# Decode attention with a gated MLP on one core: wq's first load in eight interleaved transfers, K's first head in two halves, slots at multiples of 4096 bytes

## The chip, the cores and the metric

The kernel runs on 1 core of one Trainium2 chip. The metric is the device time of one execution in microseconds (us). Before the change it is 1366.23 us, the median of 3 runs (1365.65 to 1366.27).

## The reference, cut to what matters

One token (x, 576 wide) is normalized. From the result come two sums that are added to x: attention of 32 heads over a cache of 16384 keys and values of 128 floats each, and a gated MLP (4608 wide).

```python
def _A_ref(x, k_cache, v_cache, wq, wo):          # 32 heads, Sk = 16384, Dh = 128
    q = (x @ wq).reshape(B, Sq, H, Dh).transpose(0, 2, 1, 3)
    scores = jnp.einsum("bhqd,bhkd->bhqk", q, k_cache) * (Dh ** -0.5)
    p = _softmax(scores, axis=-1)
    o = jnp.einsum("bhqk,bhkd->bhqd", p, v_cache)
    return o.transpose(0, 2, 1, 3).reshape(B, Sq, H * Dh) @ wo

def _B_ref(x, w_gate, w_up, w_down):              # 576 -> 4608 -> 576
    h = _gelu(x @ w_gate) * (x @ w_up)
    return h @ w_down

xn = _layernorm(x)
return x + _A_ref(xn, k_cache, v_cache, wq, wo) + _B_ref(xn, w_gate, w_up, w_down)
```

All is float32. K and V are 8.39 MB per head each, 537 MB together; the weights are another 51 MB. Each byte is used once.

## The kernel before, in words

Three buffers of 64 KB per partition, `slot_a`, `slot_b` and `slot_v` (called `sa`, `sb`, `sv`), lie one behind the other in SBUF from byte 27904 (`SLOT_AT`) of each partition. Everything large passes through them. All large loads are issued on SP's queue, in the order of the program text; a load waits at SP until the buffer that it overwrites has been read.

Start. The very first instruction of SP loads rows 0 to 511 of wq into `slot_a` (L127): partition p receives rows 4p to 4p+3, which are 64 KB that lie together. It stands ahead of the rest of the program and raises the semaphore `ends` by 64; PE's first instruction waits for that (L222). Behind it SP issues the last 64 rows of wq (into `slot_b`, behind the place of w_gate's main part), the small pieces of w_gate and w_up (into `slot_v`), and w_gate's main part (into `slot_b`). ACT's queue loads x. DVE normalizes x; PE turns it into a column with five small products (into `pc`), and DVE spreads that column (`z`). `project` then multiplies x by wq: one step with the last rows, four steps with those in `slot_a`. ACT takes the first head's part of q (`qcur`), PE spreads it over all partitions, ACT copies it to `qs`. When PE has read `slot_a`, w_up's main part is loaded there. `ffn(0)` and `ffn(1)` do w_gate and w_up in the same way.

Heads. K of head 0 goes to `slot_b` as soon as w_gate has been used, K of head 1 to `slot_a` behind w_up, V of head 0 to `slot_v`. Then a loop on SP (L354 to L359) issues, for each head in turn, K two heads ahead (when DVE has signalled `s_kf`, that is, read a K) and V one head ahead (when PE has signalled `s_vf`). Each of these loads is 128 partitions of 64 KB.

Each engine has its own loop over the heads, coupled by semaphores. DVE, for each head (L376 to L389): wait for K (`s_k`) and for `qs` (`s_qd`), multiply K by `qs` in place (L382), tell ACT that `qs` may be overwritten (`s_qf`), sum over the 128 floats of each key (L384), tell SP that K is free (`s_kf`), and find the maximum with PE's help (L387, L389). ACT forms the exponentials; PE multiplies them with V in 32 groups (L361 on, recorded at L329), and signals `s_vf`. The heads alternate between `slot_b` (even) and `slot_a` (odd).

End. When K of head 30 has been used, 28 rows per partition of w_down go to `slot_b`; V of head 31, the rest of w_down and wo follow in pieces. DVE sums the first part of w_down, PE the rest and wo; the last small pieces of wo end the kernel.

The class `Order` keeps the books outside the loops: each instruction and each load is noted with the partitions and elements that it touches (`box`), and `needs` works out which semaphores a later one must wait for. `load` (L217; its transfers stand at L107 in the profile, other operations at L207, L210 and L215) makes a new semaphore for each load.

Of the kernel before, what the change touches and what calls it, by code (L numbers as in the profile page):

```python
# [10 lines left out]
ALU = mybir.AluOpType  # L11
AX = mybir.AxisListType

P = 128
H, SK, DH = 32, 16384, 128
D, DF = 576, 4608
R = SK // P
SUB = 64
DJ = 4
DM = P * DJ  # L20
# [12 lines left out]
WO_A = 20  # L33
WO_Q = 8
QUART = D // 4
SLOT_AT = 27904
SLOT_B = R * DH * 4


class Order:  # L40
# [15 lines left out]
        lo = ap.offset % row  # L56
        return ap.tensor.name, ap.offset // row, ap.offset // row + parts * max(1, pstep // row), lo, lo + sum(s * (n - 1) for s, n in free) + 1

    def needs(self, eng, reads, writes):
        need = {}  # L60
        for aps, is_write in ((reads, False), (writes, True)):
            for ap in aps:
                name, p0, p1, lo, hi = self.box(ap)
                for q0, q1, l, h, wrote, who, sem, value in self.log.get(name, ()):
                    if (wrote or is_write) and q0 < p1 and p0 < q1 and l < hi and lo < h:
                        if who == eng == "tensor":
                            continue
                        if self.seen[eng].get(sem, 0) < value and need.get(sem, 0) < value:
                            need[sem] = value
        self.seen[eng].update(need)  # L70
        return list(need.items())
# [29 lines left out]
        self.note(eng, self.sem[eng], value, reads, writes)  # L101

    def dma(self, dst, src, sem, value=16, eng="sync", out=False):
        need = self.needs(eng, [src] if out else [], [] if out else [dst])
        for s, v in need[:-1]:
            getattr(self.nc, eng).wait_ge(s, v)
        i = getattr(self.nc, eng).dma_start(dst, src)  # L107
        if need:
            i._wait_ge(*need[-1])
        i.then_inc(sem, 16)  # L110
        if value and not out:
            self.note("dma", sem, value, [], [dst])
# [5 lines left out]
@with_exitstack  # L118
def kernel(ctx: ExitStack, tc: tile.TileContext, x, k_cache, v_cache, wq, wo, wg, wu, wd, out):
    nc = tc.nc  # L120
    ends = tc.alloc_semaphore("ends")
    slots = []
    for i, name in enumerate(("slot_a", "slot_b", "slot_v")):
        t = nc.alloc_sbuf_tensor_at(name, [P, R * DH], F32, offset=SLOT_AT + i * SLOT_B)
        SIZES[t.name] = R * DH
        slots.append(t.ap())
    i = nc.sync.dma_start(slots[0], wq[:DM].rearrange("(p j) f -> p (j f)", j=DJ)).then_inc(ends, 64)  # L127
    tc.no_tile_sem_insts.add(i.ins.name)
    tc.add_to_no_dep_group("first", i.ins)
    tc.declare_fence(nc.sync.nop().ins, group="first")  # L130
    with tc.tile_critical(sync_engine=mybir.EngineType.SP):
        decode(tc, x, k_cache, v_cache, wq, wo, wg, wu, wd, out, slots, ends)
    tc.no_sync_barrier()
    nc.sync.wait_ge(ends, 64)
# [19 lines left out]
def decode(tc, x, k_cache, v_cache, wq, wo, wg, wu, wd, out, slots, s_ends):  # L154
    nc = tc.nc
    o = Order(tc)
# [3 lines left out]
    def sem():  # L160
        return tc.alloc_semaphore(f"d{next(names)}")

    def sbuf(name, *shape):
        n = 1
        for s in shape[1:]:
            n *= s
        t = nc.alloc_sbuf_tensor(name, [P, n], F32)
        SIZES[t.name] = n
        return t.ap()[: shape[0]]

    def psum(name, banks):
        t = nc.alloc_psum_tensor(name, [P, 512 * banks], F32)
        SIZES[t.name] = 512 * banks
        return t.ap()

    kv, vv = (c.rearrange("b h (p n) d -> p (b h) (n d)", p=P) for c in (k_cache, v_cache))
    xf = x.rearrange("b s d -> (b s) d")
    of = out.rearrange("b s d -> (b s) d")
    wmain = {n: w[:DM].rearrange("(p j) f -> p (j f)", j=DJ) for n, w in (("q", wq), ("g", wg), ("u", wu))}
# [4 lines left out]
    sa, sb, sv = slots  # L184
# [5 lines left out]
    qcur, qs = sbuf("qcur", 1, DH), sbuf("qs", P, DH)  # L190
    S = sbuf("scores", P, 2 * R)
# [3 lines left out]
    pm, nm, nb = sbuf("pm", P, 1), sbuf("nm", P, 1), sbuf("nb", P, 1)  # L195
    small = sbuf("small", P, 32)
    oT = sbuf("oT", P, WO_T)
    assert nc.sbuf_base <= SLOT_AT, nc.sbuf_base

# [3 lines left out]
    pt, pb, pc = pg[:, 512:1024], pg[:, 1024:], psum("pc", 1)  # L203
# [5 lines left out]
    def dve(name, out, *ins, **kw):  # L209
        o.op("vector", lambda e: getattr(e, name)(out, *ins, **kw), out, *[a for a in ins if isinstance(a, bass.AP)],  # L210
             *[a for a in kw.values() if isinstance(a, bass.AP)])
# [5 lines left out]
    def load(dst, src, **kw):  # L217
        o.dma(dst, src, sem(), **kw)
        return dst

    ROW3 = 3 * DF
    nc.tensor.wait_ge(s_ends, 64).then_inc(s_ends, -64)  # L222
    qt = load(sb[:, ROW3 : ROW3 + QS], wtail["q"])
    row3, tails, at = {}, {}, 0
    for n in "gu":
# [7 lines left out]
    for i in range(2):  # L233
# [6 lines left out]
    s_q, s_m, s_n, s_o, s_e, s_v, s_po, s_pq, s_pt, s_pb, s_pc, s_vf, s_kf, s_qf, s_qd, s_d, s_a = (  # L240
        tc.alloc_semaphore(f"h{n}") for n in range(17))
    s_k = [tc.alloc_semaphore(f"k{n}") for n in range(2)]
# [45 lines left out]
    def q_part(h):  # L288
        r, lo = 32 * (h // (H // 4)), h % (H // 4) * DH
        return qb[r : r + 1, lo : lo + DH]  # L290
# [41 lines left out]
    def take(e, s, n=1):  # L332
        e.wait_ge(s, n).then_inc(s, -n)  # L333

    def head(h):
        return bass.ds(h, 1)
# [6 lines left out]
    def load_k(h, dst, s):  # L343
        nc.sync.dma_start(dst, kv[:, head(h), :].rearrange("p h f -> p (h f)")).then_inc(s_k[s], 16)
# [1 line left out]
    def load_v(h):  # L346
        nc.sync.dma_start(sv, vv[:, head(h), :].rearrange("p h f -> p (h f)")).then_inc(s_v, 16)

    for h, dst in ((0, sb), (1, sa)):
        o.wait("sync", [], [dst])  # L350
        load_k(h, dst, h)
    o.wait("sync", [], [sv])
    load_v(0)
    with nc.sync.Fori(0, (H - 2) // 2) as i:  # L354
# [18 lines left out]
               for k in range(32)], s_po)  # L373
        nc.tensor.drain().then_inc(s_vf, 1)

    with nc.vector.Fori(0, H // 2):  # L376
        for s, kt in ((0, sb), (1, sa)):
            blk = kt.rearrange("p (n d) -> p n d", d=DH)
            sc = S[:, s * R : s * R + R]
            take(nc.vector, s_k[s], 16)  # L380
            take(nc.vector, s_qd)
            nc.vector.tensor_mul(blk, blk, qs.unsqueeze(1).to_broadcast([P, R, DH])).then_inc(s_d, 1)  # L382
            nc.vector.wait_ge(s_d, 1).then_inc(s_qf, 1)
            nc.vector.tensor_reduce(sc, blk, axis=AX.X, op=ALU.add).then_inc(s_d, 1)  # L384
            nc.vector.wait_ge(s_d, 2).then_inc(s_kf, 1)
            take(nc.vector, s_d, 2)
            nc.vector.reduce_max(pm, sc, axis=AX.X).then_inc(s_m, 1)  # L387
            take(nc.vector, s_pt)
            nc.vector.tensor_reduce(nm[:1], pt[:1, :P], axis=AX.X, op=ALU.max, negate=True).then_inc(s_n, 1)  # L389

    for h0, n in ((0, 6), (6, 8), (14, 8), (22, 8), (30, 2)):
        row, lo = divmod(min(h0 + 2, H - 1), H // 4)
        with nc.scalar.Fori(0, n) as i:
# [11 lines left out]
            src = q_part(min(h0 + 2, H - 1)) if n == 2 else qb[32 * row : 32 * row + 1, bass.ds(i * DH + lo * DH, DH)]  # L405
# [102 lines left out]
```

## Time and profile before

| | |
|---|---|
| median of 3 runs | 1366.23 us |
| the profiled execution | 1364.84 us |
| its span, first to last instruction | 1363.0 us |
| DVE busy | 1158.4 us (85%) |
| PE busy | 446.3 us (33%) |
| ACT busy | 67.8 us (5%) |
| read from HBM | 587.60 MB, mean 431 GB/s |
| K load, issue to landing (median) | 42.1 us |
| V load, issue to landing (median) | 29.1 us |

How to read it: the span is what the trace covers; the time is measured around it. A row of the timeline gives start, duration, engine, line and operation, output and inputs, and in brackets how long the engine was idle before and what ended that. A `q` behind an engine's name is its instruction queue: there an SP row is the issue of a transfer, not the transfer. In the view of stretches, each row has the stretch, its length, the busy time and number of instructions of PE, PE's weight loads, DVE, ACT and POOL, then the granted clock of TensorE, the DMA share and the rate.

### The profile page before, as it was taken

The page shows a single profiled execution, that of the slowest core. Times are in us where ns is not written, and L with a number is a line of the kernel's source. Part 1 is how long each engine was busy: PE and PEld are TensorE (multiplying, and loading weights), DVE is VectorE, ACT ScalarE, POOL GpSimd, SP SyncE. Part 2 cuts the span into 40 slices and gives each one's busy share as a digit, 9 for nine tenths or more (in the row PEclk, how much of TensorE's full clock was granted, in tenths as well). Part 3 has the DMA queues.
Part 4 walks back from the last instruction along what each step waited for, and adds up shares of the span by engine and source line. Part 5 has one row for each costly group of instructions (what it writes and reads, how often), then busy time and mean ns, then how long its engine had stood idle before and what let it go on. Part 6 is the DMA issues. An engine that isn't in the chain of part 4 may idle for free. (4 is left out here: it accounts for less than half of the span.)

```text
span 1363.0 us, 7778 instructions
## 1 busy us (share of the span) xinstructions
PE 446.3 (33%) x3012; PEld 161.7 (12%) x3012; DVE 1158.4 (85%) x193; ACT 67.8 (5%) x234; POOL 1.0 (0%) x7
## 2 busy tenths in 40 slices
PE   2431233333322333323222333333223333232236
PEld 1110101111111111101111111011011111011112
DVE  1049999999998888898888888998888888988882
ACT  0000000000000000000000000000000000000000
POOL 0000000000000000000000000000000000000000
PEclk9675666666556666665566666665566666655568
DMA  9999999999999999999999999999999999999998
GB/s 401 446 424 431 431 440 437 431 435 431 435 437 431 433 431 431 446 435 431 431 439 433 433 431 431 446 435 431 431 435 437 433 431 431 444 437 431 430 437 349
DMA packets 11683, 587.69 MB, mean 431 GB/s; under 512 B 1303, under 2 KB 1309, under 8 KB 1694
## 3 DMA queue, kind: packets, MB, share of 16 engines
q1 hardware_dynamic: 11668, 587.60, 99.7%
q8 instruction: 5, 0.08, 0.0%
q10 hardware_dynamic: 10, 0.01, 0.0%
HBM read 587.60 MB, written 0.00 MB: 431 GB/s over the span
## 5 line engine op out<-in xcount | busy, mean ns | idle before, releaser
L329 PE MATMUL po<-slot_v,pe 128*4 128x512 f32 x2048 | 291.7, 733 | 532.6 <-PEq L333 532.6
L382 DVE TENSOR_TENSOR slot_b<-slot_b,qs 128x16384 f32<-128x16384 f32 x16 | 275.6, 17226 | 38.0 <-DVEq L333 38.0
L382 DVE TENSOR_TENSOR slot_a<-slot_a,qs 128x16384 f32<-128x16384 f32 x16 | 275.6, 17226 | 30.6 <-DVEq L333 30.6
L384 DVE TENSOR_REDUCE scores<-slot_a 128x128 f32<-128x16384 f32 x16 | 275.5, 17220 | 2.3
L384 DVE TENSOR_REDUCE scores<-slot_b 128x128 f32<-128x16384 f32 x16 | 275.5, 17220 | 2.3
L329 PEld LDWEIGHTS po<-slot_v,pe 128*4 128x4 f32 x2048 | 56.2, 98 | 740.9 <-issue 740.9
L365 PE MATMUL pg<-ident,pm 128*1 128x128 f32 x32 | 11.9, 371 | 287.3 <-PEq L333 287.3
L329 PE MATMUL pc<-same,z 128*128 128x1 f32 x256 | 59.8, 355 | 0.0
L395 ACT ACTIVATE z<-po 128x512 f32<-128x512 f32 x32 | 19.1, 597 | 783.1 <-ACTq L333 783.1
L329 PEld LDWEIGHTS pc<-same,z 128*128 128x128 f32 x256 | 57.1, 328 | 0.5
L210 DVE TENSOR_TENSOR slot_v<-pg,same 128x396 f32<-128x396 f32 (+1 forms) x6 | 3.3, 558 | 51.9 <-PE pg L207 51.7
L365 PEld LDWEIGHTS pg<-ident,pm 128*1 128x1 f32 x32 | 2.5, 79 | 292.6 <-issue 292.6
L389 DVE TENSOR_REDUCE nm<-pg 1x1 f32<-1x128 f32 x32 | 8.9, 279 | 21.5 <-DVEq L333 21.5
L329 PE MATMUL pg<-nm,ones 1*128 1x1 f32 x64 | 17.7, 343 | 18.5 <-PEq L333 18.5
L329 PE MATMUL pqs<-qcur,ones 1*128 1x128 f32 x64 | 14.8, 312 | 25.3 <-PEq L333 25.3
L210 DVE SCALAR_TENSOR_TENSOR slot_b<-slot_b,hT 128x576 f32<-128x576 f32 x27 | 22.1, 819 | 0.9
L400 ACT ACTIVATE nb<-pg 128x1 f32<-128x1 f32 x32 | 5.5, 171 | 292.3 <-ACTq L333 292.3
L329 PEld LDWEIGHTS pg<-nm,ones 1*128 1x128 f32 x64 | 15.9, 306 | 27.9 <-issue 27.9
L387 DVE TENSOR_REDUCE pm<-scores 128x1 f32<-128x128 f32 x32 | 9.1, 286 | 8.2 <-DVEq L333 8.2
L329 PEld LDWEIGHTS pqs<-qcur,ones 1*128 1x128 f32 x64 | 9.6, 186 | 53.9 <-issue 53.9
L207 PE MATMUL pg<-slot_b,z 128*32 128x396 f32 (+1 forms) x72 | 8.8, 661 | 17.5 <-DMA slot_b<-in_B_w_gate_dram 17.5
L402 ACT ACTIVATE pe<-scores,nb 128x128 f32 x32 | 12.8, 401 | 9.6 <-ACTq L333 9.6
(79 smaller groups left out, 115.3 us busy)
## 6 DMA issues: line engine op xcount, KB each, us to landing
slot_b<-in_B_w_down_dram SPq DMA_DIRECT2D x1, 8064.0 KB, 42.0
slot_b<-in_B_w_gate_dram SPq DMA_DIRECT2D x1, 6912.0 KB, 54.9
slot_a<-in_B_w_up_dram SPq DMA_DIRECT2D x1, 6912.0 KB, 38.2
slot_a<-in_A_wo_dram SPq DMA_DIRECT2D x1, 3456.0 KB, 41.0
slot_v<-in_B_w_gate_dram SPq DMA_DIRECT2D x1, 2304.0 KB, 28.8
slot_v<-in_B_w_up_dram SPq DMA_DIRECT2D x1, 2304.0 KB, 36.8
slot_a<-in_B_w_down_dram SPq DMA_DIRECT2D x1, 2304.0 KB, 28.1
slot_a<-in_A_wo_dram SPq DMA_DIRECT2D x1, 2304.0 KB, 33.2
```

The costliest lines, as they stand in the source:

```text
L207: o.op("tensor", lambda e: e.matmul(outp, lhsT, rhs, start=start, stop=stop), outp, lhsT, rhs, signal=signal)
L210: o.op("vector", lambda e: getattr(e, name)(out, *ins, **kw), out, *[a for a in ins if isinstance(a, bass.AP)], *[a for a in kw.values() i ...
L329: i = nc.tensor.matmul(dst, lhs, rhs, start=start, stop=stop)
L365: nc.tensor.transpose(pt[:1, :P], pm, ident).then_inc(s_pt, 1)
L382: nc.vector.tensor_mul(blk, blk, qs.unsqueeze(1).to_broadcast([P, R, DH])).then_inc(s_d, 1)
L384: nc.vector.tensor_reduce(sc, blk, axis=AX.X, op=ALU.add).then_inc(s_d, 1)
L387: nc.vector.reduce_max(pm, sc, axis=AX.X).then_inc(s_m, 1)
L389: nc.vector.tensor_reduce(nm[:1], pt[:1, :P], axis=AX.X, op=ALU.max, negate=True).then_inc(s_n, 1)
L395: nc.scalar.activation(z, PO, AF.Copy).then_inc(s_o, 1)
L400: nc.scalar.activation(nb, pb[:, :1], AF.Copy, scale=SCALE).then_inc(s_a, 1)
L402: nc.scalar.activation(pe, S[:, bass.ds(i % 2 * R, R)], AF.Exp, bias=nb, scale=SCALE, accum_out=lsum[:, bass.ds(i + h0, 1)]).then_inc(s_e, 1)
```

## The change

Three edits.

1. `SLOT_AT` goes from 27904 to 28672 (7 x 4096); the slots are 65536 bytes each, so all three now start at a multiple of 4096.
2. wq's main part comes by eight transfers. The first, at the old place, brings partitions 0, 8, ..., 120 and raises `ends`. Seven more, at the head of the other loads, bring partitions b, b+8, ... for b = 1 to 7, on one semaphore, `every`; whoever reads or overwrites `slot_a` waits for 112 on it. `needs` gets the semaphore that a load raises itself (`own`), so that the seven don't wait for one another. PE's first wait now stands for the first transfer alone.
3. K of head 0 comes in two loads of 64 keys per partition. DVE does head 0 ahead of its loop: multiply and sum of the first half, then of the second; then it frees K and `qs`. The loop on DVE runs over pairs of `slot_a` and `slot_b`, and the last head stands behind it. Heads, operations and their order stay the same otherwise.

```diff
-SLOT_AT = 27904
+SLOT_AT = 28672
+STEP = 8
...
-    def needs(self, eng, reads, writes):
+    def needs(self, eng, reads, writes, own=None):
...
-                        if who == eng == "tensor":
+                        if who == eng == "tensor" or sem is own:
                             continue
...
     def dma(self, dst, src, sem, value=16, eng="sync", out=False):
-        need = self.needs(eng, [src] if out else [], [] if out else [dst])
+        need = self.needs(eng, [src] if out else [], [] if out else [dst], sem)
...
-    i = nc.sync.dma_start(slots[0], wq[:DM].rearrange("(p j) f -> p (j f)", j=DJ)).then_inc(ends, 64)
+    i = nc.sync.dma_start(slots[0][::STEP, :], wq[:DM].rearrange("(p j) f -> p (j f)", j=DJ)[::STEP, :]).then_inc(ends, 64)
...
     nc.tensor.wait_ge(s_ends, 64).then_inc(s_ends, -64)
+    every = sem()
+    for b in range(1, STEP):
+        o.dma(sa[b::STEP, :], wmain["q"][b::STEP, :], every, 16 * (STEP - 1))
     qt = load(sb[:, ROW3 : ROW3 + QS], wtail["q"])
...
-    for h, dst in ((0, sb), (1, sa)):
-        o.wait("sync", [], [dst])
-        load_k(h, dst, h)
+    parts = [(sb[:, i * SUB * DH : (i + 1) * SUB * DH], S[:, i * SUB : (i + 1) * SUB]) for i in range(R // SUB)]
+    for i, (dst, _) in enumerate(parts):
+        load(dst, kv[:, 0, i * SUB * DH : (i + 1) * SUB * DH])
+    o.wait("sync", [], [sa])
+    load_k(1, sa, 1)
...
-    with nc.vector.Fori(0, H // 2):
-        for s, kt in ((0, sb), (1, sa)):
...
+    def highest(sc):
+        nc.vector.reduce_max(pm, sc, axis=AX.X).then_inc(s_m, 1)
+        take(nc.vector, s_pt)
+        nc.vector.tensor_reduce(nm[:1], pt[:1, :P], axis=AX.X, op=ALU.max, negate=True).then_inc(s_n, 1)
+
+    def scores_of(kt, s):
+        sc = S[:, s * R : s * R + R]
+        blk = kt.rearrange("p (n d) -> p n d", d=DH)
+        take(nc.vector, s_k[s], 16)
+        take(nc.vector, s_qd)
+        nc.vector.tensor_mul(blk, blk, qs.unsqueeze(1).to_broadcast([P, R, DH])).then_inc(s_d, 1)
+        nc.vector.wait_ge(s_d, 1).then_inc(s_qf, 1)
+        nc.vector.tensor_reduce(sc, blk, axis=AX.X, op=ALU.add).then_inc(s_d, 1)
+        nc.vector.wait_ge(s_d, 2).then_inc(s_kf, 1)
+        take(nc.vector, s_d, 2)
+        highest(sc)
+
+    take(nc.vector, s_qd)
+    for src, sc in parts:
+        blk = src.rearrange("p (n d) -> p n d", d=DH)
+        dve("tensor_mul", blk, blk, qs.unsqueeze(1).to_broadcast([P, SUB, DH]))
+        dve("tensor_reduce", sc, blk, axis=AX.X, op=ALU.add)
+    nc.vector.wait_ge(o.sem["vector"], o.count["vector"]).then_inc(s_kf, 1)
+    nc.vector.nop().then_inc(s_qf, 1)
+    highest(S[:, :R])
+    with nc.vector.Fori(0, (H - 2) // 2):
+        scores_of(sa, 1)
+        scores_of(sb, 0)
+    scores_of(sa, 1)
```

More of the change, by code (lines that the diff above doesn't have):

```diff
@@ L374, in decode @@
         nc.tensor.drain().then_inc(s_vf, 1)
-    with nc.vector.Fori(0, H // 2):
-        for s, kt in ((0, sb), (1, sa)):
[L378 to L389, printed above, removed]
+    def highest(sc):
[25 more added lines that the diff above has]
+    scores_of(sa, 1)
     for h0, n in ((0, 6), (6, 8), (14, 8), (22, 8), (30, 2)):
```

## The prediction

> **What bounds the kernel now.** I read the whole-span views first: the slices, the queues, the chain that ended last.
>
> ```profile
> span 1363.0 us, 7778 instructions
> ...
> DMA  9999999999999999999999999999999999999998
> ...
> q1 hardware_dynamic: 11668, 587.60, 99.7%
> ...
> DMA 6%; DVE 1%; PE 0%; issue 0%; DVEq 0%
> ```
>
> SP's queue q1 moves 587.60 MB and its packets fill 99.7% of the 16 engines' span; the chain that ended last consists of transfers but for 1%. To see what one packet costs I asked for the busy time of short stretches; the last two columns are the DMA share and GB/s, and both count a packet whole in the stretch where it starts.
>
> ```profile
> 0.00:1.70 1.70, 0.00 (x0) 0.00 (x0) 0.00 (x0) 0.00 (x0) 0.33 (x5) 1.00 0.00 0
> 1.70:1.80 0.10, 0.00 (x0) 0.00 (x0) 0.05 (x1) 0.00 (x0) 0.10 (x1) 1.00 1.99 655
> 2.60:2.70 0.10, 0.00 (x0) 0.00 (x0) 0.10 (x1) 0.00 (x0) 0.00 (x0) 1.00 1.80 655
> 7.20:7.30 0.10, 0.00 (x0) 0.00 (x0) 0.00 (x0) 0.00 (x0) 0.00 (x0) 1.00 1.51 655
> 19.20:19.30 0.10, 0.00 (x0) 0.00 (x0) 0.00 (x0) 0.00 (x0) 0.00 (x0) 1.00 1.51 655
> 131.50:131.60 0.10, 0.10 (x2) 0.10 (x2) 0.10 (x1) 0.00 (x0) 0.00 (x0) 0.50 7.51 2622
> 136.40:136.50 0.10, 0.10 (x4) 0.00 (x0) 0.10 (x1) 0.00 (x0) 0.00 (x0) 0.59 3.02 1311
> 424.20:462.84 38.64, 11.97 (x78) 4.38 (x77) 35.01 (x4) 1.98 (x7) 0.00 (x0) 0.63 1.00 434
> 1349.80:1352.80 3.00, 1.96 (x34) 0.83 (x36) 0.00 (x0) 0.00 (x0) 0.00 (x0) 1.00 0.99 421
> ```
>
> At 7.20 us, 655 GB/s over 0.10 us is 65.5 KB: one packet, the 64 KB that one partition receives. A share of 1.51 of 16 engines over 0.10 us is 2.42 us. The packet at 19.20, the two at 136.40 (3.02 halved) and the steady rate of a whole head (434 GB/s, 27.1 per engine) say the same: 64 KB in 2.42 us, whether DVE and PE are busy or not. The first packets of all take 3.18 us (1.99) and 2.88 us (1.80), and the 16 engines begin between 1.70 and 2.70.
>
> 587.60 MB at 434 GB/s are 1354 of the 1363.0 us. So whatever makes the transfer engines slower or idle is paid in full, and whatever only frees another engine pays nothing. To see whether the queue ever runs dry I read the issues and, beside them, who waited for the landings.
>
> ```profile
> 0.75 0.48 SPq L127 DMA_DIRECT2D slot_a<-in_A_wq_dram  x1
> 1.58 0.35 SPq L107 DMA_DIRECT2D slot_b<-in_A_wq_dram  x1
> 1.99 1.21 SPq L107 DMA_DIRECT2D slot_v<-in_B_w_gate_dram  x2
> 3.25 0.95 SPq L107 DMA_DIRECT2D slot_v<-in_B_w_up_dram  x2
> 4.24 0.45 SPq L107 DMA_DIRECT2D slot_b<-in_B_w_gate_dram  x1
> 37.25 0.33 SPq L107 DMA_DIRECT2D slot_a<-in_B_w_up_dram  x1
> 68.16 0.33 SPq L344 DMA_DIRECT2D slot_b<-in_A_k_cache_dram  x1
> 83.17 0.33 SPq L344 DMA_DIRECT2D slot_a<-in_A_k_cache_dram  x1
> 85.95 0.33 SPq L347 DMA_DIRECT2D slot_v<-in_A_v_cache_dram  x1
> 130.00 0.34 SPq L344 DMA_DIRECT2D slot_b<-in_A_k_cache_dram  x1
> ```
>
> ```profile
> 22.92 2.42 PE L207 MATMUL pc<-ones,slot_v 1*128 1x1 f32 x10 [22.92 <-PEq L222]
> ...
> 26.32 3.64 PE L207 MATMUL qb<-slot_b,z 128*32 128x512 f32 x16 [0.98 <-DVE z L210]
> ...
> 36.39 0.27 ACT L215 ACTIVATE qcur<-qb 1x128 f32<-1x128 f32 x1 [24.63 <-PE qb L207]
> ...
> 59.15 8.79 PE L207 MATMUL pg<-slot_b,z 128*32 128x396 f32 x72 [17.49 <-DMA slot_b<-in_B_w_gate_dram]
> ...
> 75.54 7.43 PE L207 MATMUL pg<-slot_a,z 128*32 128x396 f32 x72 [3.73 <-DMA slot_a<-in_B_w_up_dram]
> ...
> 95.06 17.23 DVE L382 TENSOR_TENSOR slot_b<-slot_b,qs 128x16384 f32<-128x16384 f32 x1 [7.92 <-DVEq L333]
> ```
>
> w_up is issued 21.9 us before w_gate has landed (37.25 against 59.15), K's first head 7.4 us before w_up has (68.16 against 75.54), the second head and V's first 11.9 and 9.1 us before 95.06. The one thin place is 130.00: DVE has only then finished with head 0, and the packets that follow are disturbed: the four at 131.50 took 3.0 us each (7.51 x 1.6 / 4) instead of 2.42. Later DVE catches up and waits for the transfers:
>
> ```profile
> 385.67 17.23 DVE L382 TENSOR_TENSOR slot_b<-slot_b,qs 128x16384 f32<-128x16384 f32 x1 [0.68 <-DVEq L333]
> 424.31 17.22 DVE L382 TENSOR_TENSOR slot_a<-slot_a,qs 128x16384 f32<-128x16384 f32 x1 [2.56 <-DVEq L333]
> ```
>
> Head 9 begins at 424.31, 329.25 us after head 0; the 17 transfers between those landings need 17 x 19.32 (half of 38.64) = 328.4. So about 0.8 us are lost near 130, and afterwards nothing.
>
> **The change part by part.**
>
> *wq in eighths: the packets.* Today each engine takes 8 rows of wq, 8 x 2.42 = 19.3 us. Afterwards each of eight transfers brings 16 partitions, 8 apart, one for each engine if it is spread over 16 of them, and the sum of rows is the same. What the trace doesn't show is a transfer to 16 partitions. All rows above belong to transfers to 128, where the sixteen times 27.1 GB/s can be the engines' own speed or that of sixteen ways into SBUF, each for 8 partitions. From the rows the two can't be told apart. Low end: 2.42 us stays, cost 0. High end: in each eighth, two engines write into one way while another way lies idle; each packet then takes 4.83 us, eight rounds 38.7, cost +19.3. Which one holds depends on which partitions share a way. If 0 to 7 do, then steps of 8 meet each way once; if they are grouped otherwise, some are met twice, and then in every round, since the engines go through the eighths in one order. A packet time that is the same to the hundredth at 7, 19 and 136 us speaks for a fixed width at the narrowest point and not for a queue with reserves. I take the high end, without certainty.
>
> [...]
>
> *wq in eighths: the start.* The first transfer has 16 rows to set up instead of 128. The engines that begin at 2.60 could begin with the first at 1.70: between 0 and -0.9 us, I take -0.5. SP issues seven more transfers, at 0.35 to 0.48 us some 2.5 to 3.4 us, and the eighth wq transfer comes by 5 us instead of 0.75. It is needed in the last of eight rounds, beyond 17 us. w_gate's issue goes from 4.24 to some 7 us, while its bytes start near 40. Cost 0, hidden behind the packets ahead of it; without that cover it would be 3 us.
>
> *wq in eighths: the waits.* PE's first wait ends with the first eighth, so the five small products at 22.92 go ahead as soon as x is normalized, and the 64 matmuls on slot_a wait for all seven others. Today those ten PE instructions and the copies behind them hold q up from 22.92 to 26.32: 3.4 us gained for PE. Behind it stand ACT's qcur and SP's issue of w_up, which is 21.9 us early already: worth 0. With wq 19.3 us later, q's product (10.1 us from 26.32 to 36.39) starts near 44 and ends at 54, or 64 at half speed; w_gate would land at 78.5, so w_up is still in time. All later issues and landings move by the same 19.3.
>
> *K's first head in halves.* Each half is 9.66 us of transfer, and DVE needs 17.2 us for it (half of two instructions of 17.2). It starts 9.66 earlier, ends the first half 7.6 us after the whole has landed and the second at 24.8, where now it is 34.9 (95.06 to 130.00). K's third load is issued 10 us sooner and the thin place at 130 goes: between 0 and -0.8, I take -0.6. Late next is then nothing: V's loads follow PE, which the change leaves alone. Eight packets more per engine: an engine moves 9.2 KB rows at 26.6 GB/s (421 over 0.99 x 16, at 1349.80), 346 ns each, and 64 KB in 2416 ns, so a packet has a fixed part of about 7 ns; cost 0.06 us. The copy of qs for head 1 now waits for both halves' reduction; behind it stands head 1 on DVE, at most 0.5 us late, and from 424 on DVE waits 2.56 us per head: 0.
>
> *Slots at multiples of 4096 bytes.* Every packet is a whole row whose start moves by 768 bytes. Of what could depend on that, I know only the 7 ns: 587.60 MB are 560 packets of 64 KB per engine, so at best -4 us. Rows that start elsewhere (the 9.2 KB ones) fit the same width; I take 0.
>
> Sum: +19.3 - 0.5 - 0.6 + 0.1 = **+18.3 us**. The profiled execution took 1364.84 us, 1.84 more than its span, and would take 1383.1; it lies 1.4 below the median of the runs, 1366.23. On the median: **1384.5 us**.
>
> **The rivals.**
>
> *Each engine has its own way* (not slower). The sixteen packets of an eighth run undisturbed. It decides at one point: the packets of the second round last 2.42 us and not 4.8. For it speaks that no row above has packets disturbing each other; against it, that no row has two engines writing where they could. Sum -0.5 - 0.6 + 0.1 = -1.0: 1365.2 us, within 0.2% of before (2.7 us, about what a measurement can tell from no change). This is also the case where the change doesn't do what it says: the early PE start and DVE's 10 us end in a queue that is full anyway.
>
> [...]
>
> *Ways are shared only in part*, as where one engine's gaps take in another's packet: a quarter of the doubling, +4.8 - 1.0: 1370 us.
>
> *Alignment counts*: -4 - 1.0: 1361.2 us.
>
> **How the numbers follow.** Chances: doubling 0.50, own ways 0.30, engine by partition 0.08, partly shared 0.07, alignment 0.05. The doubling's own range is 1383.4 to 1386.6: from all of both small gains (-0.9, -0.8) to neither and half a us more for first packets, and half a us at each end for the spread of the runs shown (1365.65 to 1366.27). The likeliest two lie 19 us apart, so the range must span both: 1364.0 to 1386.6, which leaves out alignment, the lower part of the second case and the ends of the first, some 0.15. Slower: 0.50 + 0.07 + 0.02 from the third case = 0.59. Faster: 0.05 + 0.03 = 0.08. Same: 0.33.
>
> **What would show it.** Short stretches of the first 45 us: packets of 4.8 us and some 217 GB/s until 41 us bear the doubling out; 2.42 and the last wq row near 22 refute it, and with it the forecast. All else should move with that: w_gate's matmuls at 78.5 or 58.5, head 0's second multiply right behind its first half's reduction, the issue of K's third load 25 us after K's second half has landed, and 3.0 us packets gone there. From head 9 on, 38.64 us per head as now; 38.5 or less would mean that alignment counts.

## The result, and the profile after

The changed kernel takes 1385.22 us (median of 4 runs, 1385.15 to 1385.42) against 1366.25 before (4 runs, 1365.65 to 1367.1): ratio 1.0142, 95% interval 1.0130 to 1.0154, that is 19.0 us slower. The profiled execution took 1385.42 us, its span is 1383.6 us.

The whole-span page of the changed kernel looks almost like the one before:

```profile
span 1383.6 us, 7786 instructions
...
DMA  9999999999999999999999999999999999999998
GB/s 212 366 428 446 430 430 443 430 430 438 436 428 436 440 428 430 445 428 428 447 428 428 447 428 426 449 428 426 449 428 426 447 426 430 447 426 430 444 429 344
...
q1 hardware_dynamic: 11924, 587.60, 99.6%
...
DMA 6%; DVE 1%; PE 0%; issue 0%
```

The transfer engines are as busy as before (99.6% against 99.7%), with the same 587.60 MB. The busy share doesn't show the loss here: the GB/s row does, and only in its first two slices (34.6 us each), 212 and 366, where the same row of the kernel before begins with 401 and 446:

```profile
GB/s 401 446 424 431 431 440 437 431 435 431 435 437 431 433 431 431 446 435 431 431 439 433 433 431 431 446 435 431 431 435 437 433 431 431 444 437 431 430 437 349
```

The view of short stretches of the changed kernel, as in the prediction (the last two columns are DMA share and GB/s, a packet counts whole where it starts), shows where the loss arises:

```profile
2.10:2.20 0.10, 0.00 (x0) 0.00 (x0) 0.01 (x2) 0.00 (x0) 0.10 (x1) 1.00 11.58 2621
3.30:3.40 0.10, 0.00 (x0) 0.00 (x0) 0.10 (x1) 0.10 (x1) 0.00 (x0) 1.00 2.84 655
6.80:6.90 0.10, 0.00 (x0) 0.00 (x0) 0.00 (x0) 0.00 (x0) 0.00 (x0) 1.00 3.20 655
11.90:12.00 0.10, 0.10 (x2) 0.10 (x1) 0.00 (x0) 0.00 (x0) 0.00 (x0) 1.00 3.20 655
22.20:22.30 0.10, 0.00 (x0) 0.00 (x0) 0.00 (x0) 0.00 (x0) 0.00 (x0) 1.00 3.08 655
27.10:27.20 0.10, 0.00 (x0) 0.00 (x0) 0.00 (x0) 0.00 (x0) 0.00 (x0) 1.00 3.21 655
30.00:40.00 10.00, 0.00 (x0) 0.00 (x0) 0.00 (x0) 0.00 (x0) 0.00 (x0) 1.00 1.03 210
444.62:483.28 38.66, 12.66 (x77) 4.45 (x77) 35.01 (x4) 1.98 (x7) 0.00 (x0) 0.59 1.00 434
```

One packet of 64 KB (655 GB/s over 0.10 us) now has a share of 3.20, that is 5.12 us, where it had 1.51 and 2.42 us. Sixteen of them are under way at a time, and together they move 205 GB/s until wq is in (16 x 65.5 KB in 5.12 us; the row from 30 to 40 us has 210, because it counts packets whole). A head later on takes 38.66 us at 434 GB/s, as before. What stands behind wq is moved as a block; these are rows of the timeline of the changed kernel (SP's issues, PE, DVE):

```profile
0.75 0.67 SPq L128 DMA_DIRECT2D slot_a<-in_A_wq_dram  x1
1.76 4.29 SPq L108 DMA_DIRECT2D slot_a<-in_A_wq_dram  x7
10.43 2.45 PE L208 MATMUL pc<-ones,slot_v 1*128 1x1 f32 x10 [10.43 <-DVE slot_v L211]
46.49 3.64 PE L208 MATMUL qb<-slot_b,z 128*32 128x512 f32 x16 [33.62 <-DMA slot_b<-in_A_wq_dram]
58.20 0.33 SPq L108 DMA_DIRECT2D slot_a<-in_B_w_up_dram  x1
80.43 7.31 PE L208 MATMUL pg<-slot_b,z 128*32 128x396 f32 x72 [17.82 <-DMA slot_b<-in_B_w_gate_dram]
104.60 0.33 SPq L348 DMA_DIRECT2D slot_a<-in_A_k_cache_dram  x1
108.37 0.20 DVE L211 SCALAR_TENSOR_TENSOR hT<-tt,gu 128x36 f32<-128x36 f32 x1
108.57 8.69 DVE L211 TENSOR_TENSOR slot_b<-slot_b,qs 128x8192 f32<-128x8192 f32 x1
143.65 0.35 SPq L348 DMA_DIRECT2D slot_b<-in_A_k_cache_dram  x1
```

PE's five small products start at 10.43 instead of 22.92, and then PE waits 33.62 us for wq. w_gate's matmuls start at 80.43, 21.3 us later than before. K's third load is issued 39.1 us after its second (104.60, 143.65), where it was 46.8 (83.17, 130.00). The last matmul of the kernel before started at 1359.22 us, that of the changed one at 1379.54: 20.3 us, so of those 21.3 one us has been won back on the way.

```profile
1359.22 0.43 PE L207 MATMUL pg<-slot_b,oT 128*1 128x144 f32 x8 [0.29 <-DMA slot_b<-in_A_wo_dram]
```

```profile
1379.54 0.43 PE L208 MATMUL pg<-slot_b,oT 128*1 128x144 f32 x8 [0.25 <-DMA slot_b<-in_A_wo_dram]
```

### The profile page after: what moved, and what is told of

It reads as the page before. It is cut to its first block, busy times and chain, and to the rows that moved or that the text cites. A ratio compares the mean times of both kernels' runs of the same rounds, so it can differ in the third digit from the quotient of the medians.

```text
span 1383.6 us, 7786 instructions
## 1 busy us (share of the span) xinstructions
PE 446.6 (32%) x3012; PEld 161.1 (12%) x3012; DVE 1158.7 (84%) x195; ACT 67.9 (5%) x234; POOL 1.0 (0%) x7
## 3 DMA queue, kind: packets, MB, share of 16 engines
q1 hardware_dynamic: 11924, 587.60, 99.6%
HBM read 587.60 MB, written 0.00 MB: 425 GB/s over the span
## 5 line engine op out<-in xcount | busy, mean ns | idle before, releaser
L392 DVE TENSOR_TENSOR slot_b<-slot_b,qs 128x16384 f32<-128x16384 f32 x15 | 258.4, 17226 | 33.6 <-DVEq L337 33.6
L394 DVE TENSOR_REDUCE scores<-slot_b 128x128 f32<-128x16384 f32 x15 | 258.3, 17220 | 2.2
L211 DVE TENSOR_REDUCE scores<-slot_b 128x64 f32<-128x8192 f32 x2 | 17.4, 8686 | 0.1
L211 DVE TENSOR_TENSOR slot_b<-slot_b,qs 128x8192 f32<-128x8192 f32 x2 | 17.4, 8686 | 0.0
```

## The experiments

The theory is that of the forecast: in every eighth, two engines write into one way of SBUF. No view shows a way; what is measured is the time of a packet, 2.42 us in the kernel before and 5.12 in the changed one. Its rivals after the result: the loss comes from one of the other two edits; from the reads, whose rows now lie 512 KB apart in HBM; or from the number of rows in a transfer, whichever they are. Each is the changed kernel, the one before, or an earlier experiment with one edit.

### e1: wq in one transfer, the other two edits kept

```diff
-    i = nc.sync.dma_start(slots[0][::STEP, :], wq[:DM].rearrange(...)[::STEP, :]).then_inc(ends, 64)
+    i = nc.sync.dma_start(slots[0], wq[:DM].rearrange(...)).then_inc(ends, 64)
...
-    every = sem()
-    for b in range(1, STEP):
-        o.dma(sa[b::STEP, :], wmain["q"][b::STEP, :], every, 16 * (STEP - 1))
```

> The changed kernel with wq's main part in one transfer to 128 partitions again; K's first head in halves and the slots at multiples of 4096 stay. Theory (two engines write into one way of SBUF in every eighth): the whole loss goes, 64 KB packets of the first 22 us take 2.42 us again, no disturbed packets when K's third load starts; time 1365.6 us, 0.6 below before. Rival (a part of the loss comes from the halves or the new slot places): between 1367 and 1385.

Measured: 1363.94 us (1363.80 to 1364.16) against 1365.89 before, ratio 0.9986 (0.9977 to 0.9995). The whole loss goes, so it lies in the eighths alone: 1385.22 - 1363.94 = 21.3 us (the two medians come from different sets of runs, in which the kernel before differs by 0.4 us). The other edits win 1.95 us by the medians, three times what the theory said.

### e2: only the slots moved

```diff
-SLOT_AT = 27904
+SLOT_AT = 28672
```

> The kernel before with only its slots moved to multiples of 4096 bytes. Theory (a packet costs its bytes and 7 ns, wherever its row starts): 1366.2 us, 38.64 us per head from head 9 on. Rival (the place of a row counts): at least 1 us off, in every head alike, 38.6 us or less per head.

Measured: 1365.92 us against 1365.89, ratio 1.000 (0.9991 to 1.0010). The place of a row is worth nothing that can be measured.

### e3: only K's first head in halves

```diff
 # from the changed kernel as in e1, and
-SLOT_AT = 28672
+SLOT_AT = 27904
```

> The kernel before with only K's first head in halves. Theory (the thin place at 130 us is worth 0.6): K's third load is issued some 27 us after K's second half has landed instead of 35, its first packets take 2.42 us, time 1365.6. Rival (the queue was not empty there, the slower packets only waited for memory): 1366.2, and the first packets of that load still take 2.8 us or more.

Measured: 1363.96 us (1363.79 to 1364.05) against 1365.89, ratio 0.9987 (0.9978 to 0.9996). The halves win 1.9 us, not 0.6, and the runs, which spread over 2.4 us before (1364.54 to 1366.91), now spread over 0.3. The issue of K's third load in this kernel, and the short stretch in which its packets begin (the same stretch stands in e9 below):

```profile
123.02 0.35 SPq L345 DMA_DIRECT2D slot_b<-in_A_k_cache_dram  x1
```

```profile
131.40:131.60 0.20, 0.00 (x0) 0.00 (x0) 0.20 (x1) 0.00 (x0) 0.00 (x0) 0.50 6.07 2622
```

2622 GB/s over 0.20 us are 8 packets; 6.07 x 16 x 0.20 / 8 is 2.43 us for each. The load was issued 7.0 us earlier than in the kernel before (123.02 against 130.00), while V's first was still on its way; so the engines pass from one to the other, and nothing is disturbed.

### e9: the halves, but DVE begins only when both are there

```diff
 # from e3
     take(nc.vector, s_qd)
+    o.wait("vector", [sb])
     for src, sc in parts:
```

> e3 (K's first head in halves, all else as before), but DVE begins head 0 only when both halves have landed. Theory (the halves gain because K's third load is issued before the queue runs dry): the issue falls back to 35 us after K's landing, its first packets are disturbed again (2.6 us and more), and the 1.9 us are lost: 1365.9. Rival (the smaller packets, or one load more, gain the time): 1364.0, and no disturbed packets.

Measured: 1365.65 us (1364.76 to 1366.68) against 1365.72, ratio 0.9999 (0.9990 to 1.0008). The gain is gone, and the spread of 1.9 us is back. DVE's first multiply and SP's next issues in this kernel, and the short stretch:

```profile
94.99 8.69 DVE L211 TENSOR_TENSOR slot_b<-slot_b,qs 128x8192 f32<-128x8192 f32 x1 [6.71 <-DMA slot_b<-in_A_k_cache_dram]
```

```profile
84.32 0.33 SPq L345 DMA_DIRECT2D slot_a<-in_A_k_cache_dram  x1
87.11 0.33 SPq L348 DMA_DIRECT2D slot_v<-in_A_v_cache_dram  x1
130.08 0.35 SPq L345 DMA_DIRECT2D slot_b<-in_A_k_cache_dram  x1
```

```profile
131.40:131.60 0.20, 0.20 (x2) 0.20 (x2) 0.20 (x1) 0.00 (x0) 0.00 (x0) 0.50 4.30 1639
```

The third load is issued at 130.08 again, and its first packets take 2.75 us (4.30 x 3.2 / 5). So neither the smaller transfers nor the extra one win the time; the earlier issue of K's third load, and of the loads that follow from it, does.

Why does this win 1.9 us in the median, when the trace of before shows 0.8? The profiled executions lie at different places in the spread: e3's took 1363.92 us, before's 1364.84, e2's (the same order of loads as before) 1365.50 and e9's 1366.68. DVE's head 9 waits for its K in all of them; it begins at 424.31 in before (the row is in the prediction), and in e3, e2 and e9, in this order, at

```profile
423.54 17.23 DVE L389 TENSOR_TENSOR slot_a<-slot_a,qs 128x16384 f32<-128x16384 f32 x1 [2.60 <-DVEq L334]
```

```profile
424.92 17.23 DVE L382 TENSOR_TENSOR slot_a<-slot_a,qs 128x16384 f32<-128x16384 f32 x1 [2.52 <-DVEq L333]
```

```profile
425.12 17.22 DVE L389 TENSOR_TENSOR slot_a<-slot_a,qs 128x16384 f32<-128x16384 f32 x1 [2.65 <-DVEq L334]
```

So the late issue costs 0.8, 1.4 and 1.6 us by then, and the forecast had the mildest of the three to read. Nor is all of it lost at 130 us: of the packets of 64 KB behind 45 us, none takes more than 2.43 us in e3, while before has 22 of more than 2.5, 11 of them between 125 and 150 us and 9 between 200 and 300. e9 loses 1.1 us more in the last 60 us, where its engines stop out of step: 2 us before its last large packet ends, 5 packets are under way, and in e3 all 16 engines are still at work. Why packets take longer so far behind the late load, and why some executions suffer more than others, stays open.

### e4: eighths of 16 neighbouring partitions

```diff
+ROWS = P // STEP
...
-        o.dma(sa[b::STEP, :], wmain["q"][b::STEP, :], every, 16 * (STEP - 1))
+        o.dma(sa[b * ROWS : (b + 1) * ROWS, :], wmain["q"][b * ROWS : (b + 1) * ROWS, :], every, 16 * (STEP - 1))
```

The first transfer likewise takes partitions 0 to 15.

> The changed kernel with each eighth made of 16 neighbouring partitions instead of every eighth one; the rows of wq that go there lie together in HBM too. [...] Rival 1 (the reads: rows 512 KB apart in HBM disturb each other): neighbours lie 64 KB apart, packets of 2.42 us, 1366. Rival 2 (a transfer of 16 rows is slow as such, whichever they are): packets of 5.1 us, 1385.

Measured: 1419.38 us (1419.18 to 1419.48), ratio 1.0391 (1.0375 to 1.0407). A short stretch of this kernel:

```profile
66.90:67.00 0.10, 0.00 (x0) 0.00 (x0) 0.00 (x0) 0.00 (x0) 0.00 (x0) 1.00 11.74 1311
```

Two packets, 11.74 x 1.6 / 2 = 9.4 us each: nearly four times 2.42. It is as many rows per transfer as in the changed kernel, and they lie closer in HBM, but it is 34 us slower; both rivals fall. Read by the theory, four engines share a way here.

### e5: destination as in the change, reads from neighbouring rows

```diff
-        o.dma(sa[b::STEP, :], wmain["q"][b::STEP, :], every, 16 * (STEP - 1))
+        o.dma(sa[b::STEP, :], wmain["q"][b * ROWS : (b + 1) * ROWS, :], every, 16 * (STEP - 1))
```

> The changed kernel, every eighth partition as destination, but each transfer reads 16 rows that lie together in HBM (64 KB apart instead of 512 KB), so that wq's rows meet the wrong entries of x: the product x times wq is not the reference's. Theory (the ways into SBUF): nothing changes, packets of 5.1 us, 1385. Rival (the reads in steps of 512 KB): packets of 2.42 us, 1366.

Measured: 1385.46 us (1385.43 to 1385.52), ratio 1.0146 (1.0129 to 1.0163), and in this kernel's stretches

```profile
12.00:12.10 0.10, 0.10 (x2) 0.10 (x2) 0.00 (x0) 0.00 (x0) 0.00 (x0) 1.00 3.21 655
30.00:40.00 10.00, 0.00 (x0) 0.00 (x0) 0.00 (x0) 0.00 (x0) 0.00 (x0) 1.00 1.02 210
```

the same 5.1 us and 210 GB/s. Whether the rows come from places 64 or 512 KB apart doesn't matter here.

### e6, e7, e8: 64 neighbours, every second, every fourth partition

```diff
 # e6, from e4             # e7, from the change     # e8, from the change
-STEP = 8                 -STEP = 8                 -STEP = 8
+STEP = 2                 +STEP = 2                 +STEP = 4
```

> wq in two transfers, partitions 0 to 63 and 64 to 127, four rows per engine. [...] Rival 1 (the number of rows per transfer counts, 16 being too few): 64 rows are nearly like 128, packets of 2.42 us, 1366. Rival 2 (the partition fixes the engine): 8 engines per transfer, packets of 2.42 us, both transfers at once, some 1367.

> [...] What counts is which four rows an engine gets. If in order (rows 4i to 4i+3 of the transfer, partitions 8i, 8i+2, 8i+4, 8i+6), the 16 engines are on 8 ways at any time, packets of 5.1 us, 1385. If the rows are dealt out so that each engine stays on a way of its own, 2.42 us and 1366. Rival to the ways (a transfer slows with its number of rows): packets between 2.42 and 5.1 us.

> [...] If an engine gets its rows in order (partitions 8i and 8i+4) or in two rounds (4i, then 64+4i), 8 ways at any time, packets of 5.1 us, 1385. If each engine stays on a way of its own, 2.42 us and 1366. Rival (a transfer slows with its number of rows): between e7 and the changed kernel.

Measured against 1365.59 before: e6 1385.30 us (1385.18 to 1385.48), ratio 1.0145 (1.0128 to 1.0162); e7 1364.55 (1364.41 to 1364.89), ratio 0.9993 (0.9984 to 1.0003); e8 1364.87 (1364.68 to 1364.97), ratio 0.9992 (0.9983 to 1.0002). A stretch of each, in this order:

```profile
12.30:12.40 0.10, 0.00 (x0) 0.00 (x0) 0.00 (x0) 0.00 (x0) 0.00 (x0) 1.00 12.82 2621
```

```profile
12.70:12.80 0.10, 0.00 (x0) 0.00 (x0) 0.07 (x2) 0.00 (x0) 0.00 (x0) 1.00 10.62 4588
```

```profile
12.70:12.80 0.10, 0.10 (x3) 0.10 (x2) 0.00 (x0) 0.00 (x0) 0.00 (x0) 1.00 3.03 1311
```

Four packets at 5.13 us in e6, seven at 2.43 in e7, two at 2.42 in e8. e6 and e7 move 64 rows per transfer, in two transfers; they differ only in which rows. e8 moves 32, in four transfers, and its packets are as fast as those of one transfer of 128 rows (2.42 us). So the number of rows explains nothing here, nor does the number of transfers (two in e6 cost what eight cost in the change); which partitions are under way at one time explains all of it.

Together the runs fix the grouping as far as they reach. Counted from the packet times, with one engine on a way at 2.42 us, sixteen neighbours put four engines on a way (9.4 us, e4), 64 neighbours and every eighth partition two (5.13, e6; 5.12, the changed kernel), every second and every fourth one (2.43, e7; 2.42, e8). So some neighbours share a way, and so do some partitions that lie a multiple of 8 apart. Which ones do, beyond this, was not shown.

## Why the prediction was right

*The doubling.* Right as far as packet times tell: they follow the partitions that are under way at one time (9.4, 5.13, 2.43 and 2.42 us in e4, e6, e7 and e8). Right in place too (the packets of the second round, e1). No row of the kernel before showed which partitions share a way; the high end was the author's choice. Mis-sized: the forecast took packets to last 4.83 us; they last 5.12, and the eighths cost 21.3 us by e1 instead of 19.3 less 0.5. The 5.12 is some 6% beyond the doubling, and the forecast had no row from which to expect that.

*The start.* Wrong in sign. The term was -0.5 us because 16 rows should be set up sooner than 128. SP needs 0.67 us for the first transfer where it needed 0.48, and the engines begin between 2.10 and 3.40 instead of 1.70 and 2.70. So it costs 0.4 to 0.7 us, which is part of the 21.3. It isn't the number of rows alone: 16 neighbours in e4 take 0.46, 64 in e6 take 0.62. What sets it stays open.

*The waits.* Right. PE's small products run 12.5 us earlier and nothing comes of it; w_up's issue at 58.20 is still 22.2 us ahead of w_gate's matmuls at 80.43. e7 and e8 give PE an early start too (13.66 and 10.69 us, against 10.43 in the changed kernel) without the doubling, and lie 0.6 and 0.9 us above e1 (measured in another set of runs).

*K's halves.* Right in mechanism (e9), too small. The term was -0.6 us, worked out from one trace; e3 measures -1.9 by the medians. The step that failed is the one from the profiled execution to the median: it was one of the fastest of a kernel whose runs spread over 2.4 us, and the thin place is what spreads them; the traces of e2 and e9 show 1.4 and 1.6 us by head 9 where that one shows 0.8. The forecast's "near 130, and afterwards nothing" was off too: a part of the 0.8 goes between 200 and 300 us (e9). One further step was off without consequence: DVE starts the first half at 108.57, right behind the last MLP product at 108.37, which w_up's landing sets; so K's third load comes 7.8 us sooner (39.1 against 46.8), not 10.

*The slots.* Right: e2.

*The sum.* +18.3 was forecast and +19.0 measured, which looks better than it is: the eighths cost 2.5 us more than forecast, the halves win 1.3 more. That the time lies in the stated range says little in itself, since the range (1364.0 to 1386.6) was made to span the two likeliest cases; it is the packet times that tell them apart.

The rival of own ways, at 0.30, fell to e4 and e6, and that of the partition fixing the engine too: in e6 it would have packets of 2.42 us, and they take 5.13. No run shows a time for that case; its 0.02 in the chance of slower was the author's estimate. The rival of ways shared only in part would have packets near 3.0 us (a quarter of the doubling), and falls with the 5.12 of the changed kernel; that of alignment falls with e2.

*A version that beats both.* e1 and e3, at 1363.94 and 1363.96 us: the halves without the eighths. They are within 0.1 of each other, so the slots' place may be as it is.

## What to carry to other kernels

Read GB/s and the time of a single packet beside the DMA share: here the share was 1.03 while wq came at 210 GB/s (packets of 5.12 us), and 1.00 in a head at 434 (2.42 us). When a transfer is cut into parts of fewer partitions, choose the parts by the packet time that they give: every second or fourth partition kept the 2.42 us here (2.43 and 2.42, e7 and e8), every eighth and 64 neighbours took 5.12 and 5.13, and sixteen neighbours 9.4. And where a stream is the bound, look for the one place where its next transfer is issued too late; closing it won 1.9 us here where its trace showed 0.8, and the runs spread over 0.3 us instead of 2.4 (e3).

## What the runs showed of the hardware that was not expected

Four engines on a way move more together than two, by the count above: 16 packets of 65.5 KB per 9.4 us are 112 GB/s, 28 for each four engines (e4), while packets of 5.12 us make 205 GB/s, 25.6 for each two (the changed kernel). One engine alone on its way has 27.1 (64 KB in 2.42 us). Why four move more than two, no run shows.

In e7 and e8 the rows are not dealt out to the engines in their order, nor in rounds of 16 by the order of the partitions; both were expected as possible. In their order, partitions 8 apart would have been under way together, as in the changed kernel (5.12 us); in rounds of 16, those of one half, as in e6 (5.13). The transfers of 32 and 64 spread rows have packets of 2.42 and 2.43 us, so by the count above each engine stays on a way of its own. How the rows are dealt can't be read from these traces.

In the changed kernel one round of packets is shorter: 3.08 at 22.20, 4.93 us, between rounds of 5.1. It is the fifth; why, no run shows.
